# A gated attention + GLU kernel on one core: the five engines' instructions emitted into the program's main body instead of a block

## The chip, the core and the metric

The kernel runs on one core of one Trainium2 chip. The core has five engines with instruction streams of their own: TensorE (PE, with its weight loads listed apart as PEld), ScalarE (ACT), VectorE (DVE), GpSimd (POOL) and SyncE (SP). They meet only at semaphores. The metric is device time in microseconds (us) of one launch; lower is better.

## What is computed

One layer with two branches that share the input `x` (2048 rows of 512, bf16). Branch A is attention in four segments of 512 rows, with 32 heads of 16 and a running memory `M`, `z` of the earlier segments; branch B is a GLU with tanh-GELU, 1792 wide. A sigmoid gate per row mixes them.

```python
g = sigmoid((x * gate_w).sum(-1, keepdims=True))
# A, for each segment s of 512 rows, for each head:
a_dot = softmax(qs @ ks.T * 0.25 + causal_mask) @ vs
a_mem = (phi(qs) @ M) / (phi(qs) @ z + 1e-6)
o     = sigmoid(beta) * a_mem + (1 - sigmoid(beta)) * a_dot
M, z  = M + phi(ks).T @ vs, z + phi(ks).sum(rows)
a     = concat(o) @ wo
# B:
b = (gelu(x @ w_gate) * (x @ w_up)) @ w_down
out = g * a + (1 - g) * b
```

## The kernel before

`_build` (L428 on) works in two steps. First it makes a graph of some 1,200 tasks: the K, Q and V projections, the score matmuls (`fill`, L867), the exponentials (L878), the masks (L881, POOL), the products with V (`pv`, L914), the normalisation (`norm`, L937), the gate, up and down matmuls of the GLU, and the DMAs. The order in which each engine takes its tasks is written out by hand, one list for each engine (`ORDER`, L41). `Sched.schedule` (L238) walks those lists once with estimated durations; the walk decides which of four PSUM banks a group of matmuls gets. `em.plan` (L1116) and `em.finalize` (L1117) then turn the dependences into semaphore waits. All of that is done before the first instruction is emitted.

Second, it emits the streams. `Emitter.emit_stream(eng)` (L395) takes the planned list of one engine and emits, for each entry, its waits (L399) and the instruction itself. It always emits on `engmap[eng]`, the same five engine objects, wherever it is called from.

Before, the five calls stand inside `with nc.Block() as block:` (L1120). Each decorated function (L1121 to L1141) is the body of one engine, a piece of code of its own: in the program as written, each engine branches from the main body into its piece, runs it, and branches to a common end, where the block puts an all-engine barrier. In that barrier every engine drains (waits for its own instructions to retire); SP, ACT, DVE and PE each raise a semaphore; POOL waits for the four, then raises another semaphore that the four wait for. SP's body has seventeen more waits behind its last DMA (L1140, L1141): the fifteen outputs of 128 rows, and the two column pieces in which the last 128 rows are written (`sem_tail` and the last `sem_out`).

Ahead of all this the main body holds what the framework puts there when the program is opened (L1173): four constant memsets on POOL and an all-engine barrier of the same shape. The change does not touch it.

The last work of the program: PE finishes the last tile's matmuls in two column pieces (`on_x`, L1034); ACT scales the first piece into `pex` (L1048), DVE the second into `obf` (L1051), and SP writes both to memory (L1053).

Of the kernel before, what the change touches and what calls it, by code (L numbers as in the profile page):

```python
# [7 lines left out]
PE, ACT, DVE, POOL, SP = "pe", "act", "dve", "pool", "sp"  # L8
# [414 lines left out]
def build(nc, A_x, A_wq, A_wk, A_wv, A_wo, A_beta, B_x, B_w_gate, B_w_up, B_w_down, gate_w, out):  # L423
    with ExitStack() as es:
        return _build(es, nc, A_x, A_wq, A_wk, A_wv, A_wo, A_beta, B_w_gate, B_w_up, B_w_down, gate_w, out)


def _build(es, nc, A_x, A_wq, A_wk, A_wv, A_wo, A_beta, B_w_gate, B_w_up, B_w_down, gate_w, out):  # L428
# [61 lines left out]
    em = Emitter(nc, engmap)  # L490
    nsem = [0]

    def sem(name):
        nsem[0] += 1
        return es.enter_context(nc.semaphore(f"{name}_{nsem[0]}"))
# [581 lines left out]
    sem_out = [sem("so") for _ in range(16)]  # L1077
    sem_tail = sem("st")
# [38 lines left out]
    em.finalize()  # L1117
    nc._sched = S

    with nc.Block() as block:  # L1120
        @block.gpsimd  # L1121
        def _(e):
            em.emit_stream(POOL)

        @block.scalar
        def _(e):
            em.emit_stream(ACT)

        @block.vector
        def _(e):  # L1130
            em.emit_stream(DVE)

        @block.tensor
        def _(e):
            em.emit_stream(PE)

        @block.sync
        def _(e):
            em.emit_stream(SP)
            for sm in sem_out[:-1] + [sem_tail, sem_out[-1]]:  # L1140
                e.wait_ge(sm, 16)  # L1141


def bass_gated_mix__memory_aug_infini_attn__glu_gated_geglu__prompt_kernel(
# [43 lines left out]
```

## Time and profile before

| | us |
|---|---|
| median of 3 runs | 266.35 |
| lowest and highest of them | 266.17, 298.27 |
| profiled execution: span from first to last instruction | 264.8 |
| the same execution's own device time | not recorded apart from its span |

Busy time in that span: PE 256.1 us (97%), ACT 209.0 (79%), DVE 197.5 (75%), POOL 105.7 (40%). The granted TensorE clock is 1.000 throughout.

How to read the profile: "L503" is line 503 of the kernel. An engine's name with a q (SPq, PEldq) is its sequencer, the part that waits, branches and issues DMAs; its instructions aren't counted as busy. The view of one line lists every kind of instruction of that line: how many, the duration in ns (lowest/median/highest), and when the first and the last started, in us from the start of the span. The chain of waits follows the work that ended last back to what released it. A time line lists instructions as start, duration, engine, line.

### The profile page before, as it was taken

The page shows a single profiled execution, that of the slowest core. Times are in us where ns is not written, and L with a number is a line of the kernel's source. Part 1 is how long each engine was busy: PE and PEld are TensorE (multiplying, and loading weights), DVE is VectorE, ACT ScalarE, POOL GpSimd, SP SyncE. Part 2 cuts the span into 40 slices and gives each one's busy share as a digit, 9 for nine tenths or more (in the row PEclk, how much of TensorE's full clock was granted, in tenths as well). Part 3 has the DMA queues.
Part 4 walks back from the last instruction along what each step waited for, and adds up shares of the span by engine and source line. Part 5 has one row for each costly group of instructions (what it writes and reads, how often), then busy time and mean ns, then how long its engine had stood idle before and what let it go on. Part 6 is the DMA issues. An engine that isn't in the chain of part 4 may idle for free.

```text
span 264.8 us, 7355 instructions
## 1 busy us (share of the span) xinstructions
PE 256.1 (97%) x3115; PEld 117.9 (45%) x3153; DVE 197.5 (75%) x376; ACT 209.0 (79%) x179; POOL 105.7 (40%) x256
## 2 busy tenths in 40 slices
PE   8999999999999999999999999999999999999996
PEld 4644444444444434443544444343444434443453
DVE  0778788989997968889897776779887751475661
ACT  3688988998999788798877987888787777786702
POOL 8206686352600067165300274609480107362410
PEclk9999999999999999999999999999999999999999
DMA  7972216900004893320003251300000021301002
GB/s 224 310 183 43 42 24 155 284 4 0 2 9 113 227 182 73 64 82 0 2 0 59 64 140 24 83 2 20 5 2 0 2 63 41 80 2 42 22 0 82
DMA packets 32769, 18.25 MB, mean 69 GB/s; under 512 B 20576, under 2 KB 32736, under 8 KB 32736
## 3 DMA queue, kind: packets, MB, share of 16 engines
q1 hardware_dynamic: 31632, 16.73, 26.2%
q10 hardware_dynamic: 1104, 1.05, 1.3%
q8 instruction: 25, 0.41, 0.7%
q14 instruction: 8, 0.07, 0.1%
HBM read 9.84 MB, written 2.10 MB: 45 GB/s over the span
## 4 chain that ended last, share of the span: by engine, by line
PE 91%; DVE 3%; issue 2%; DMA 1%; ACT 1%; DVEq 0%; ACTq 0%
PE psW L503 71%; PE psXALL L872 8%; PE psW L920 5%; PE psXALL L503 3%; DMA hT<-in_A_x_dram 1%; PE psW L928 1%; PE psW L839 1%; DVE hT L520 1%; ACT pt L878 1%; PE psXALL L599 1%; PE psXALL L792 1%; ACT L878 0%; DVE kpad L738 0%; DVE pex L700 0%; DVE phq L698 0%
## 5 line engine op out<-in xcount | busy, mean ns | idle before, releaser
L878 ACT ACTIVATE pt<-psXALL 128x2048 bf16<-128x2048 f32 x64 | 120.1, 1876 | 27.1 <-PE psXALL L872 23.5
L881 POOL TENSOR_SCALAR_AFFINE_SELECT pt<-pt 128x256 bf16<-128x256 bf16 x128 | 58.8, 471 | 103.0 <-ACT pt L878 98.2
L503 PE MATMUL psW<-xT,wu 128*128 128x512 bf16 x217 | 53.9, 380 | 0.9 <-issue 0.6
L503 PE MATMUL psW<-wd,hT 128*128 128x512 bf16 x204 | 52.8, 380 | 1.0 <-issue 0.8
L503 PE MATMUL psW<-xT,wg 128*128 128x512 bf16 x214 | 52.1, 379 | 1.4 <-issue 0.8
L1019 DVE TENSOR_TENSOR hT<-psW,hT 128x512 bf16<-128x512 f32 x56 | 36.8, 683 | 16.5 <-PE psW L503 16.2
L881 POOL TENSOR_SCALAR_AFFINE_SELECT ptl<-ptl 128x512 bf16<-128x512 bf16 x32 | 22.5, 702 | 38.3 <-ACT ptl L878 36.6
L503 PEld LDWEIGHTS psW<-xT,wu 128*128 128x128 bf16 x224 | 20.3, 98 | 25.7 <-issue 2.7
L503 PEld LDWEIGHTS psW<-xT,wg 128*128 128x128 bf16 x224 | 20.6, 98 | 24.6 <-issue 2.1
L934 DVE STREAM_TRANSPOSE tb<-psW 128x512 f32<-128x512 f32 x32 | 21.5, 699 | 11.7 <-PE psW L928 11.5
L503 PEld LDWEIGHTS psW<-wd,hT 128*128 128x128 bf16 x210 | 19.3, 98 | 23.9 <-issue 3.0
L872 PE MATMUL psXALL<-qT,kpad 32*128 32x320 bf16 (+3 forms) x512 | 25.4, 273 | 0.0
L1003 ACT ACTIVATE hT<-psW 128x512 bf16<-128x512 f32 x28 | 15.7, 596 | 5.5 <-PE psW L503 5.4
L503 PE MATMUL psW<-xT,wk 128*128 128x512 bf16 (+1 forms) x79 | 18.9, 343 | 0.2 <-DVE mzacc L850 0.2
L920 PE MATMUL psW<-pt,vaug 128*17 128x192 bf16 (+3 forms) x512 | 18.8, 273 | 0.0
L872 PEld LDWEIGHTS psXALL<-qT,kpad 32*128 32x128 bf16 x512 | 7.6, 92 | 24.5 <-ACT pt L878 15.4
L503 PE MATMUL psW<-wv,xT 128*128 128x512 bf16 x61 | 17.8, 380 | 0.5 <-issue 0.3
L878 ACT ACTIVATE ptl<-psXALL 128x2048 bf16<-128x2048 f32 x8 | 15.0, 1876 | 3.8 <-PE psXALL L872 3.6
L503 PE MATMUL psW<-wo,oT 128*128 128x512 bf16 x54 | 15.4, 380 | 1.0 <-issue 0.8
L1068 DVE TENSOR_SCALAR ost<-psW,omgt 128x512 bf16<-128x512 f32 x9 | 6.7, 746 | 11.9 <-PE psW L503 11.9
L520 DVE CAST hT<-psW 128x512 bf16<-128x512 f32 x19 | 12.8, 684 | 3.7 <-PE psW L503 3.5
L779 POOL COPY exsT<-exs 32x4 f32<-32x4 f32 x64 | 13.9, 216 | 3.7
(104 smaller groups left out, 301.8 us busy)
## 6 DMA issues: line engine op xcount, KB each, us to landing
out_dram<-ost SPq DMA_DIRECT2D x15, 128.0 KB, 1.9
wg<-in_B_w_gate_dram SPq DMA_DIRECT2D x2, 896.0 KB, 7.6
wu<-in_B_w_up_dram SPq DMA_DIRECT2D x2, 896.0 KB, 6.9
wd<-in_B_w_down_dram SPq DMA_DIRECT2D x2, 896.0 KB, 7.0
phkt<-in_A_x_dram SPq DMA_DIRECT2D x3, 512.0 KB, 4.9
vlow<-vaug SPq DMA_DIRECT2D x8, 136.0 KB, 2.8
hT<-in_A_x_dram SPq DMA_DIRECT2D x2, 256.0 KB, 3.8
wq<-in_A_wq_dram SPq DMA_DIRECT2D x2, 256.0 KB, 5.3
```

What stands on the lines that cost most here:

```text
L503: return Instr(lambda e: e.matmul(view(), lhsT, rhs, start=first, stop=last), reads=reads, writes=[fkey if fkey is not None else g.key], e ...
L520: alts[DVE] = [Instr(lambda e: e.tensor_copy(dst(), src()), reads=reads, writes=writes, est=dve_t(n))]
L599: task(f"x0t{nm}_{u}", PE, [Instr(lambda e, k=k, a=a, u=u, k0=k0, src=src: e.transpose(src[:, k, a * 128:(a + 1) * 128], xin[:, 2 * u + a, ...
L779: cross = task(f"exsT{s}", POOL, [Instr(lambda e, g=g, c=c: e.tensor_copy(exsT[sl][32 * g:32 * g + 32, c:16:4], exs[32 * c:32 * c + 32, s4 ...
L872: instrs.append(Instr(lambda e, g=g, lhs=lhs, rhs=rhs, c0=c0, ncol=ncol: e.matmul(X[g][:, c0:c0 + ncol], lhs(32 * g), rhs(32 * g), start=T ...
L878: exp_task(s, f"exp{s}_{t}{name}", [Instr(lambda e: e.activation(dst[:], XALL[:, :].rearrange("p (g c) -> p g c", g=4), ACTF.Exp, scale=AT ...
L881: task(f"msk{s}_{t}{name}", POOL, [Instr(lambda e, view=view, pat=pat, base=base: e.affine_select(out=view, in_=view, compare_op=ALU.is_ge ...
L920: instrs.append(Instr(lambda e, t=t, q=q, kb=kb, slot=slot, c0=c0: e.matmul(gp.f32()[32 * q:32 * q + 17, 128 * kb + 64:512], Vaug[sl][:, k ...
L934: task(f"pvt{s}_{t}_{j}", DVE, [Instr(lambda e: e.transpose(Tb[:, j, :], gp.f32()[:, :]), [gp.key], [("Tb", j)], dve_t(512))], grp=gp)
L1003: lambda e, g=g, ft=ft, s=s: e.activation(hT[s % 2][:, ft, :], g.f32()[:, :], ACTF.Gelu_apprx_tanh),
L1019: task(f"Um{s}_{ft}", DVE, [Instr(lambda e, g=g, ft=ft: e.tensor_tensor(hT[sl][:, ft, :], g.f32()[:, :], hT[sl][:, ft, :], ALU.mult), [g.k ...
L1068: DVE: [Instr(lambda e, view=view, gt=gt, tile=tile: e.tensor_scalar(ostage[(4 * s + tile) % N_OST][:], view(), omgt[:, gt:gt + 1], None, ...
```

## The change

The block is gone. The same five streams are emitted one after another into the main body, and SP's waits for the outputs follow as the last instructions of SP's stream. Nothing else of the program differs: the same planned lists, the same waits, the same order on every engine. With the block go its branches and its closing barrier (a drain on each of five engines, and six semaphore instructions).

```diff
-    with nc.Block() as block:
-        @block.gpsimd
-        def _(e):
-            em.emit_stream(POOL)
-
-        @block.scalar
-        def _(e):
-            em.emit_stream(ACT)
-
-        @block.vector
-        def _(e):
-            em.emit_stream(DVE)
-
-        @block.tensor
-        def _(e):
-            em.emit_stream(PE)
-
-        @block.sync
-        def _(e):
-            em.emit_stream(SP)
-            for sm in sem_out[:-1] + [sem_tail, sem_out[-1]]:
-                e.wait_ge(sm, 16)
+    for eng in (SP, ACT, PE, DVE, POOL):
+        em.emit_stream(eng)
+    for sm in sem_out[:-1] + [sem_tail, sem_out[-1]]:
+        nc.sync.wait_ge(sm, 16)
```

## The prediction

> **What bounds the kernel now.** I read the page first, then the chain of waits, then the two ends of the program, since the change touches only those. The page:
>
> ```profile
> span 264.8 us, 7355 instructions
> PE 256.1 (97%) x3115; PEld 117.9 (45%) x3153; DVE 197.5 (75%) x376; ACT 209.0 (79%) x179; POOL 105.7 (40%) x256
> q8 instruction: 25, 0.41, 0.7%
> q14 instruction: 8, 0.07, 0.1%
> PE 91%; DVE 3%; issue 2%; DMA 1%; ACT 1%; DVEq 0%; ACTq 0%
> ```
>
> TensorE bounds it: it is busy for 97% of the span, and 91% of the chain of work that ended last is its matmuls. No edit of this change adds, removes or moves a matmul, an activation or a DMA. What can move is the start (how soon the engines begin after the opening barrier), the end (how soon the program is over after the last output has landed) and, in between, only the place of each stream in the instruction memory. I take the three in turn.
>
> **The start.** The first instructions of the program, from the view of L1173 (the framework's opening barrier) and the time line:
>
> ```profile
> L1173 POOLq EVENT_SEMAPHORE  x2: 17/17/17, 0.6 to 0.7; - x2
> L1173 ACTq DRAIN  x1: 8/8/8, 0.1 to 0.1; - x1
> L1173 SPq EVENT_SEMAPHORE  x1: 17/17/17, 0.7 to 0.7; - x1
> L1173 PEldq EVENT_SEMAPHORE  x1: 51/51/51, 0.7 to 0.7; - x1
> ...
> 0.80 0.20 POOL L561 MEMSET ident<- 128x128 bf16 x1 [0.29 <-POOLq L1173]
> 0.81 1.28 ACT L565 ACT_TABLE_LOAD   x1 [0.81 <-PEq L1173]
> 0.81 0.97 SPq L534 DMA_DIRECT2D hT<-in_A_x_dram  x2
> 0.81 0.14 PEld L590 LDWEIGHTS psW<-const-bfloat16-1.0 128*128 128x128 bf16 x2 [0.81 <-issue]
> ```
>
> The engines pass the opening barrier at 0.7 and begin the block's work at 0.80 to 0.81. The branch into the block would have to fit between. The lines of the block itself hold this:
>
> ```profile
> nothing on L1121; most used: ['L503', 'L872', 'L920', 'L928', 'L839', 'L792', 'L881', 'L399', 'L878', 'L779', 'L1019', 'L534', 'L520', 'L530', 'L599', 'L934', 'L517', 'L1003', 'L1173', 'L590', 'L946', 'L948', 'L950', 'L952', 'L767']
> L1120 POOLq EVENT_SEMAPHORE  x2: 17/17/17, 264.6 to 264.7; - x2
> L1120 POOLq DRAIN  x1: 797/797/797, 251.9 to 251.9; - x1
> L1120 PEldq DRAIN  x1: 1622/1622/1622, 260.8 to 260.8; - x1
> L1120 ACTq DRAIN  x1: 611/611/611, 261.7 to 261.7; - x1
> L1120 DVEq DRAIN  x1: 393/393/393, 262.5 to 262.5; - x1
> L1120 SPq COMPARE_BRANCH  x1: 41/41/41, 264.4 to 264.4; - x1
> L1120 SPq DRAIN  x1: 7/7/7, 264.5 to 264.5; - x1
> L1120 SPq EVENT_SEMAPHORE  x1: 17/17/17, 264.7 to 264.7; - x1
> L1120 ACTq EVENT_SEMAPHORE  x1: 17/17/17, 264.7 to 264.7; - x1
> L1120 DVEq EVENT_SEMAPHORE  x1: 21/21/21, 264.7 to 264.7; - x1
> L1120 PEldq EVENT_SEMAPHORE  x1: 51/51/51, 264.7 to 264.7; - x1
> ```
>
> The trace records a branch when one is executed: SP's at 264.4, 41 ns long. It records none at the start, on any engine, and none at the end of POOL's, ACT's, DVE's or PE's stream. So the ten branches of the source have shrunk to one; the others lead to the code that lies next on that engine anyway, and the bodies are simply entered. Removing an entry branch that isn't executed is worth 0. The bound on the other side is the gap itself: SP's wait starts at 0.7 (0.65 to 0.75 before rounding) and lasts 17 ns, its first DMA issue starts at 0.81, so the gap is 0.04 to 0.14 us, and no more than 0.1 us of it can be anything but the usual step from one instruction to the next. I take 0, with -0.1 kept for the range.
>
> [...]
>
> **The end.** The last of the chain and of SP's queue:
>
> ```profile
> 260.66 1.77 PE psXALL L503 x20
> 262.46 0.35 DVE obf L1051
> ...
> 262.84 0.33 SPq L534 DMA_DIRECT2D out_dram<-obf  x1
> ...
> out_dram<-obf SPq DMA_DIRECT2D x1, 32.0 KB, 1.4
> ...
> L1141 SPq EVENT_SEMAPHORE  x8: 28/28/28, 263.2 to 264.3; - x8
> ```
>
> PE ends at 262.4, DVE writes the last piece, SP issues its DMA at 262.84, and that lands 1.4 us later, at 264.3; the last of SP's eight wait instructions (each holds two of the seventeen waits) starts then. The seventeenth wait rides on the branch at 264.4. From here on everything belongs to the block: branch, SP's drain at 264.5, POOL's gather and release at 264.6 and 264.7, the four engines' waits at 264.7, of which PE's 51 ns end the span at 264.8.
>
> Step by step: (1) SP's branch, 41 ns, goes, and a plain wait for the same semaphore takes its place, 28 ns by the L1141 row: -0.01. (2) The stretch from the branch's end, 264.44, to 264.8 goes: -0.36. Steps 1 and 2 make 264.8 - 264.4 - 0.03 = 0.37; all starts are rounded to 0.1, so 0.3 to 0.5; I take 0.4. (3) The drains of POOL, ACT, DVE and PE go: 0. They end at 252.7, 262.3, 262.9 and 262.4, each behind its own engine's last instruction with nothing queued behind it but the barrier. What hides them is SP's wait for the output until 264.3; the landing would have to come 1.4 us earlier before the latest of them showed. (4) SP's own drain, 7 ns, is inside step 2. (5) The order of emission in the source (SP first, POOL last, instead of POOL first, SP last): 0, since each engine has its own stream and the order inside each is unchanged.
>
> What is late next is the landing of the last output, 264.3, and the wait that sees it. So the span should end at 264.4.
>
> **Between.** The streams keep their instructions but may move by a few places relative to the pieces in which code is fetched. The q8 row is that fetching: 25 packets of 0.41 MB together, one for every (3115 + 3153) / 25 = 251 PE instructions recorded. Whether PE ever waits for it shows in its waits and in its densest stretch:
>
> ```profile
> PEld psW L503 <- issue: 11.4, 54, 0.2
> PEld psXALL L872 <- issue: 4.0, 10, 0.4
> PEld psW L920 <- issue: 3.4, 11, 0.4
> ...
> 111.40:114.30 2.90, 2.90 (x108) 1.59 (x107) 2.02 (x4) 2.35 (x2) 0.41 (x1) 1.00 0.26 11
> ```
>
> After the start, no wait that nothing explains is longer than 0.4 us, and in the densest stretch that I found, 215 matmuls and weight loads in 2.9 us, PE is busy for 2.90 of 2.90. So no fetch is late now. A shift by one branch per stream, even five places, moves a fetch by 5 x 264.8 / 6268 = 0.2 us. I take 0 for it, and price the other case among the rivals.
>
> **The sum.** The page gives the profiled execution's span alone, 264.8; the median of the runs, 266.35, is 1.55 above it, which I carry over as what lies around the span. 264.8 - 0.4 + 1.55 = 265.95. The gain is 0.15%, far below 2%, which is about what a measurement of this kernel can tell from no change.
>
> **The rivals.**
>
> (a) The part around the span shrinks too. Four engines now reach their program's end at 252 to 263 instead of 264.8, and whatever closes the launch could start on them early. For it: the 1.55 us exist and no row shows what fills them. Against it: the launch is over only when the last engine is, and SP is still at 264.4. Price: between 0 and all of it, 265.95 down to 264.4; the middle is 265.2. [...]
>
> (b) Nothing is gained. What follows the program may need those same 0.4 us for its own purposes, such as draining the engines that no longer drain in the kernel. POOL's drain, at 797 ns the longest that follows its engine's work, shows that a drain isn't free, but it would run in the shadow of SP's wait. Price: 266.35.
>
> (c) The first table load moves. ACT's table load (0.81, 1.28 us) stands at the top of ACT's body. If in a single body it is put at the top of the program, ahead of the opening barrier, ACT's drain at 0.1 waits for it until 1.4, and the barrier, which now takes from the last arrival (POOL's gather, 0.6) to 0.81, releases at 1.6: +0.8. Price 265.95 + 0.8 = 266.75. Against it: the load belongs to L565, the first activation.
>
> (d) The other side: fetches become late. One mechanism, on PE: a shifted piece boundary falls so that PE runs out of fetched code before the next piece is in. [...] Against it: no late fetch now, and a shift of 0.2 us at most against 2.9 us for the densest stretch.
>
> **How the numbers follow.** Chances: the forecast 0.63; (a) 0.15; (b) 0.09; (c) 0.05; (d) 0.08. The time predicted is the forecast's, 265.95. Its own range is 265.65 to 266.15: the rounding of step 2 (0.1 either way), the -0.1 of the entry, and 0.2 for the two close runs, 266.17 and 266.35. For 8 in 10 I leave out (d) and the lower part of (a): from 265.0, just under the middle of (a), to 266.9, just over (c); that takes in (b). Faster by over 2% would need 5.3 us, and no row offers more than 0.4 + 1.55; I keep 0.01 from (a) for what lies outside every row. Slower by over 2% is (d) with more than 4 late fetches, 0.07 of its 0.08. Within 2%: 0.92.
>
> **What would show it.** Right: no instruction on the block's line; about 11 fewer instructions (12 of L1120 gone, one wait more); SP's last wait ending the span near 264.4, right behind the landing of the last output; PE's and ACT's first work still at 0.8; PE's busy time still 256. Step 3 is wrong if the span ends on an engine other than SP. Wrong at the start: the first DMA issue well off 0.81, or the table load before the opening drain (c). Wrong in between: PE waits for "issue" of over 1 us, with the q8 count unchanged (d). If the span falls by 0.4 and the time doesn't, it is (b); if the time falls by more than the span, (a).

## The result, and the profile after

The changed kernel takes 265.31 us (median of 16 runs, 264.99 to 266.71), the kernel before 266.71 (16 runs, 265.96 to 298.27): a ratio of 0.9944, with a 95% interval of 0.9923 to 0.9966; runs in a slower state, such as the one of 298.27, are left out of the ratios. That is 0.9 to 2.1 us faster, well within the 2% that the prediction called no change. In a second comparison, on one chip, the ratio was 0.9966 (0.9943 to 0.9989). Both hold the 0.95 us that the sections below account for. The time lies in the predicted range of 265.0 to 266.9, but below the forecast's own range of 265.65 to 266.15. The gain is more than twice the 0.4 us of the sum, and half of it comes from a place that the sum had carried over unchanged.

The page after, its first rows:

```profile
span 264.1 us, 7382 instructions
PE 261.1 (99%) x3153; PEld 117.6 (45%) x3153; DVE 197.5 (75%) x376; ACT 209.0 (79%) x179; POOL 105.7 (40%) x256
q8 instruction: 25, 0.41, 0.7%
```

The count rises from 7355 to 7382 though the program has shrunk: all 3153 matmuls are recorded here, and 3115 were before. 7355 + 38 = 7393, and the 11 fewer that the prediction counted make 7382. For the same reason PE's busy time reads 261.1 and not 256.1; PE does the same work.

The last of the chain of waits, the time line of SP's last DMA, and the view of L1123, where SP's last waits now stand:

```profile
260.43 1.77 PE psXALL L503 x20
262.20 0.03 issue
262.22 0.35 DVE obf L1051
...
262.60 0.33 SPq L534 DMA_DIRECT2D out_dram<-obf  x1
...
L1123 SPq EVENT_SEMAPHORE  x9: 17/28/28, 263.0 to 264.1; - x9
```

Nothing follows the last wait. By the trace's events the last output lands at 264.045 and the span ends at 264.089: 0.044 us, where before it was 0.477 (264.281 to 264.758). That is the gain at the end, 0.43 us.

The span fell by 0.67, though. The other 0.23 is in the chain's rows: PE's last piece starts at 260.43, before at 260.66. It arose in the first 7 us. The time lines there, of the kernel before and then of the changed one:

```profile
6.13 0.51 PEld L503 LDWEIGHTS psW<-xT,wk 128*128 128x128 bf16 x4
7.18 0.42 DVE L607 COPY xT<-psXALL 128x512 bf16<-128x512 bf16 x1 [0.28 <-PE psXALL L599]
```

```profile
0.80 1.28 ACT L565 ACT_TABLE_LOAD   x1 [0.80 <-PEq L1155]
0.81 0.96 SPq L534 DMA_DIRECT2D hT<-in_A_x_dram  x2
0.81 0.14 PEld L590 LDWEIGHTS psW<-const-bfloat16-1.0 128*128 128x128 bf16 x2 [0.81 <-issue]
6.03 0.37 PEld L503 LDWEIGHTS psW<-xT,wk 128*128 128x128 bf16 x4
6.95 0.42 DVE L607 COPY xT<-psXALL 128x512 bf16<-128x512 bf16 x1 [0.24 <-PE psXALL L599]
```

ACT, POOL, SP and PE's loads start as before, at 0.80 and 0.81, and the copy at L607 is already 0.23 early. Four weight loads take 0.37 us instead of 0.51: in the trace of before, loads still follow one another 107 ns apart at 6.2, and are 56 ns apart first at 6.76; in this one they are 107 ns apart up to 4.97, and 56 ns first at 5.92. The traces' own records of the granted clock begin in between, with 1.0, at 6.397 us before and at 5.905 here; ahead of them nothing is recorded, and the views print 1.00 there as well. So the clock of 1.000 throughout, given with the profile before, is known only from 6.4 us on. By the first record, TensorE's step from loads 107 ns apart to loads 56 ns apart came 0.49 us earlier in this execution, and an estimate from these figures, 0.49 x (1 - 56/107) = 0.23, is the whole difference.

That isn't the change's doing: the kernel before, profiled again (`a_block`), also has its last piece early (its last weight load starts at 261.92, the changed kernel's at 261.91, before it was 262.14), and its span is 264.5. From the copy on, in the changed kernel's profile, every stage of PE, ACT and DVE stands 0.23 us early, to within 0.02, up to the last matmul. In all fourteen profiles of this study the time from PE's 61st weight load, which starts at 10.8 to 12.9 us, to its last is 250.93 to 250.95 us.

So spans compare badly from run to run: here the head moved one by 0.23. What compares well is the distance between two events of the same run: from the last landing to the span's end, and from the span to the execution's own time, which the runs after the prediction record.

### The profile page after: what moved, and what is told of

It is laid out like the page before. It is cut to its first block, busy times and chain, and to the rows that moved or that the text cites. A ratio compares the mean times of both kernels' runs of the same rounds, so it can differ in the third digit from the quotient of the medians.

```text
span 264.1 us, 7382 instructions
## 1 busy us (share of the span) xinstructions
PE 261.1 (99%) x3153; PEld 117.6 (45%) x3153; DVE 197.5 (75%) x376; ACT 209.0 (79%) x179; POOL 105.7 (40%) x256
## 4 chain that ended last, share of the span: by engine, by line
PE 96%; DMA 1%; ACT 1%; DVE 0%; issue 0%; ACTq 0%
PE psW L503 75%; PE psXALL L872 9%; PE psW L920 6%; PE psXALL L503 3%; PE psW L928 1%; DMA hT<-in_A_x_dram 1%; PE psW L839 1%; ACT pt L878 1%; PE psXALL L792 1%; PE psXALL L599 1%; ACT L878 0%; DVE obf L1051 0%; ACTq L399 0%
## 5 line engine op out<-in xcount | busy, mean ns | idle before, releaser
L503 PE MATMUL psW<-xT,wu 128*128 128x512 bf16 x224 | 55.2, 380 | 0.0
L503 PE MATMUL psW<-xT,wg 128*128 128x512 bf16 x224 | 54.2, 380 | 0.0
L503 PE MATMUL psW<-wd,hT 128*128 128x512 bf16 x210 | 54.1, 380 | 0.0
L934 DVE STREAM_TRANSPOSE tb<-psW 128x512 f32<-128x512 f32 x32 | 21.5, 699 | 11.7 <-PE psW L928 11.5
L503 PE MATMUL psW<-wv,xT 128*128 128x512 bf16 x64 | 18.5, 380 | 0.0
L503 PE MATMUL psW<-wo,oT 128*128 128x512 bf16 x60 | 16.8, 380 | 0.0
```

Source lines behind the costliest of these rows:

```text
L503: return Instr(lambda e: e.matmul(view(), lhsT, rhs, start=first, stop=last), reads=reads, writes=[fkey if fkey is not None else g.key], e ...
L934: task(f"pvt{s}_{t}_{j}", DVE, [Instr(lambda e: e.transpose(Tb[:, j, :], gp.f32()[:, :]), [gp.key], [("Tb", j)], dve_t(512))], grp=gp)
```

## The experiments

The theory: the block cost its closing barrier and SP's branch, 0.43 us inside the span. The rivals: the part around the span shrinks as well, since four engines end early; and, what exceeds 0.43 is scatter of the head. Each kernel starts from the changed kernel, but for `a_block` and `k_no_drain`, which start from the kernel before. The part around the span, which most expectations speak of, is a run's own time less its span; spans are on record to 0.1 us, so a single run gives it to 0.05. The third column is from one profile each. `a_block` to `d_all_wait` ran on one chip, `e_last_act` to `h_last_pool` on a second, the rest on a third, each beside runs of the kernel before. Here is what they gave together, in us:

| kernel | late at the end | span's end behind last landing | part around the span: median (range, runs) |
|---|---|---|---|
| before | all five, barrier | 0.477 | 1.76 (1.67 to 1.87, 97) |
| `a_block`: before again | all five, barrier | 0.477 | 1.80 (1.72 to 1.85, 12) |
| changed | SP | 0.044 | 1.26 (1.19 to 1.36, 16) |
| `b_main`: changed again | SP | 0.044 | 1.25 (1.19 to 1.35, 12) |
| `c_main_bar` | all five, barrier | 0.296 | 1.76 (1.68 to 1.80, 12) |
| `d_all_wait` | all five | 0.079 | 1.78 (1.72 to 1.86, 12) |
| `e_last_act` | ACT | 0.059 | 1.42 (1.36 to 1.43, 10) |
| `f_last_dve` | DVE | 0.075 | 1.34 (1.30 to 1.41, 10) |
| `g_last_pe` | PE | 0.079 | 1.48 (1.46 to 1.63, 10) |
| `h_last_pool` | POOL | 0.066 | 1.81 (1.73 to 1.91, 10) |
| `i_three_wait` | SP, ACT, DVE, PE | 0.079 | 1.53 (1.46 to 1.62, 10) |
| `j_two_bars` | all five, two barriers | 0.633 | 1.76 (1.68 to 1.84, 10) |
| `k_no_drain` | all five, barrier | 0.559 | 1.78 (1.67 to 1.82, 10) |
| `l_entry` | SP | 0.045 | 1.30 (1.19 to 1.36, 10) |

The times of whole runs tell these kernels apart badly. Their ratios to the kernel before are 1.0007 for `d_all_wait`, 0.9969, 0.9972, 0.9989 and 0.9992 for `e_last_act` to `h_last_pool`, and 0.9987, 0.9999, 0.9997 and 0.9988 for `i_three_wait` to `l_entry`, each with an interval of 0.001 to 0.003 either way.

**The control and the change, on one chip.**

> The kernel before, unchanged, as a control. Theory (the closing barrier alone): ratio 1.000 to the kernel before, within 0.3%; span 264.6 to 265.1, ending on PE's wait of the barrier about 0.43 us behind the last output's wait. Rival 1 (the part around the span shrank as well): the execution's own time stands about 1.5 us above its span, where the changed kernel's stands 1.2 above. Rival 2 (the rest is scatter of the head's loads): 1.2 here too, and the spans of several runs differ by 0.2 and more.

> The changed kernel again, beside the control on one chip. Theory: 0.4 to 0.5 us under the control, ratio 0.998. Rival 1: 0.7 us or more under it, ratio 0.997 or less, with the own time 1.2 above the span. Rival 2: spans differ from the control's by 0.44 at the end and by anything from -0.3 to 0.3 in the first 10 us.

The control's ratio was 1.0007 (0.9985 to 1.0029), the change's 0.9966 (0.9943 to 0.9989); their medians 266.30 and 265.54, their lowest times 265.95 and 265.23. The part around the span is 1.80 and 1.25: rival 1 holds, beside the theory. The part around shrank by 1.80 - 1.25 = 0.55 here, and by 1.76 - 1.26 = 0.50 between the two larger sets of runs; with the middle, 0.52, the accounted gain is 0.43 + 0.52 = 0.95. The two medians differ by 0.76, since the control's spans ran from 264.2 to 266.6 and the changed kernel's from 264.0 to 266.5. That is scatter of the size that rival 2 expects, and it hits both kernels.

**One barrier, no block.**

```diff
     for sm in sem_out[:-1] + [sem_tail, sem_out[-1]]:
         nc.sync.wait_ge(sm, 16)
+    nc.all_engine_barrier()
```

> The changed kernel with one all-engine barrier behind its last waits, no block. Theory: the barrier is all that the block cost, so the end is back at 0.43 us behind the last output's wait, less what SP's branch took (41 ns and the step behind it, 0.13): 0.25 to 0.45 us over the changed kernel. A rival, that the block's form (its labels and pieces of code) costs and not its barrier: ratio as the changed kernel's, within 0.1 us.

The view of the barrier's line:

```profile
L1124 POOLq EVENT_SEMAPHORE  x2: 17/17/17, 266.1 to 266.2; - x2
L1124 POOLq DRAIN  x1: 792/792/792, 253.6 to 253.6; - x1
L1124 SPq DRAIN  x1: 7/7/7, 266.1 to 266.1; - x1
L1124 PEldq EVENT_SEMAPHORE  x1: 51/51/51, 266.2 to 266.2; - x1
```

They are the rows of the block's end, without the branch. The end is 0.296 behind the landing: the barrier costs 0.25 inside the span, and the other 0.18 of the block's 0.477 is SP's branch and the step behind it. The part around is back at 1.76, and the ratio at 1.000 (0.9983 to 1.0018). The new order of emission is still in this kernel, so it isn't what shrank the part around. Inside the span the 0.25 is at the low edge of what was expected; by the medians this kernel is 0.78 over the changed one, since the part around came back too, which this expectation hadn't counted. The rival, no cost without the block's form, is refuted; the form's own share is the 0.18.

This profile also shows one case of the scatter. Its span is 266.3, 2.2 us above the changed kernel's; 0.25 of that is the barrier, and 1.93 is there at the 61st weight load:

```profile
9.23 0.60 PE L503 MATMUL psW<-xT,wk 128*128 128x256 bf16 x4 [1.98 <-DMA wk<-in_A_wk_dram]
...
wk<-in_A_wk_dram ACTq DMA_DIRECT2D x1, 256.0 KB, 7.3
```

One load of `wk` took 7.3 us from issue to landing, where the kernel before shows 5.0 for it, and PE waited 1.98 us. From the 61st weight load on, here at 12.9 us, the run is like every other.

**All wait, nothing is exchanged.**

```diff
+    for e in (nc.scalar, nc.vector, nc.tensor, nc.gpsimd):
+        e.wait_ge(sem_out[-1], 16)
```

> The changed kernel, with ACT, DVE, PE and POOL each waiting at their end for the last output's semaphore, without barrier and drains. All five engines end together, as with the block, but nothing is exchanged. Theory: span as the changed kernel's, within 0.1 us. Rival 1 (the part around the span shrank since four engines end early): own time 0.2 to 0.4 us further above the span than the changed kernel's, like the control's. If the part around stays at 1.2, early ends don't matter.

```profile
L1125 POOLq EVENT_SEMAPHORE  x1: 17/17/17, 263.9 to 263.9; - x1
L1125 PEldq EVENT_SEMAPHORE  x1: 51/51/51, 263.9 to 263.9; - x1
```

No barrier, no drain, and the end only 0.079 behind the landing; yet the part around is 1.78, the block's, and 0.53 above the changed kernel's where rival 1 had 0.2 to 0.4. That settles rival 1: without an exchange the part around is the block's (1.78 against 1.76), so it is not the exchange that costs there, it is that engines come late.

**One engine late at a time.** The seventeen last waits move from SP to another engine, so SP ends with its last DMA issue and the other alone stays:

```diff
-        nc.sync.wait_ge(sm, 16)
+        nc.scalar.wait_ge(sm, 16)
```

and in the same way with `nc.vector`, `nc.tensor` and `nc.gpsimd`.

> The changed kernel with the seventeen last waits on ACT instead of SP: ACT alone ends late. Theory (each engine has a closing piece of its own behind its stream, and the last one done sets the time): the part around the span is ACT's piece, somewhere up to 1.78, and over the four kernels of this kind the largest is 1.78. Rival (only several late engines together cost more, in a chain from engine to engine): 1.25 here as with SP alone, within 0.1. Span 263.8 to 264.2 by both, plus what the head's loads scatter.

> The same with DVE alone late. Theory: DVE's own piece, up to 1.78; a value under 1.25 would make this a faster kernel than the changed one. Rival: 1.25 within 0.1.

> The same with PE alone late. PE's wait takes 51 ns where SP's takes 28, so the span may be 0.02 longer. Theory: PE's own piece, up to 1.78. Rival: 1.25 within 0.1.

> The same with POOL alone late. POOL's own work ends at 252.4, so it stands in the waits from then on. Theory: POOL's own piece, up to 1.78; I hold POOL for the likeliest of the four to have the largest, as its drain of 797 ns in the block's barrier was the longest behind finished work. Rival: 1.25 within 0.1.

SP 1.25, DVE 1.34, ACT 1.42, PE 1.48, POOL 1.81: the price depends on the engine that is late, and POOL's alone is the 1.76 to 1.80 of all five together. The rival, 1.25 for each, is refuted by POOL (1.73 at the lowest) and PE (1.46). SP and DVE lie close: SP's median is 1.25 to 1.30 on three sets of runs, and its range, 1.19 to 1.36, overlaps DVE's. But none is below SP's, and no other engine's wait ends sooner behind the landing than SP's 0.044, so SP is already the engine to end on: `f_last_dve`, the nearest, has 0.9972 (0.9961 to 0.9982) of the kernel before, not to be told from the changed kernel.

**Four late engines, without POOL.**

```diff
+    for e in (nc.scalar, nc.vector, nc.tensor):
+        e.wait_ge(sem_out[-1], 16)
```

> The changed kernel with ACT, DVE and PE also waiting for the last output's semaphore, POOL not. Theory (the largest closing piece among the engines that end late: SP 1.25, DVE 1.34, ACT 1.43, PE 1.49, POOL 1.81): the part around the span is PE's, 1.49 within 0.05. Rival (late engines add up): over 1.6.

1.53, for 1.49 expected: close to the largest of the four, and under the 1.6 of the rival. Without POOL among the late ones, a quarter of a microsecond of the half is back.

**Two barriers, another kind of barrier, and one at the entry.** The second barrier is one more line like that of `c_main_bar`. `k_no_drain` is the kernel before with `nc.Block(no_gpsimd_drain=True)`. `l_entry` puts this ahead of the streams:

```diff
+    with nc.Block() as block:
+        for reg in (block.gpsimd, block.scalar, block.vector, block.tensor, block.sync):
+            @reg
+            def _(e):
+                pass
     for eng in (SP, ACT, PE, DVE, POOL):
```

> Two all-engine barriers behind the last waits. Theory: the second costs inside the span what the first did, 0.25, or somewhat more since POOL's drain comes anew, so the span ends 0.55 to 0.65 behind the last landing; the part around the span stays at 1.78, since POOL was late already. Rival (the part around grows with each barrier): 2.3.

> The block again, in its form with plain drains and a barrier of semaphores alone. Theory: the drains were hidden, so nothing is won by their form: the span ends 0.45 to 0.6 behind the last landing (one more semaphore instruction per engine), the part around is 1.78. Rival (the drains cost): the end closer than 0.4.

> The changed kernel with an empty block ahead of the streams: its branches and its barrier at the entry, none at the end. Theory: a barrier costs its 0.25 wherever it stands on the path, here ahead of the first loads, so the first DMA issue moves from 0.81 to 1.05 or 1.1 and the whole run with it; the branches add nothing; the part around the span is 1.25. Rival (a branch at the entry costs a fetch of code): the first issue at 2 or later.

Two barriers: 0.633 and 1.76, both as the theory has it. The first barrier costs 0.25 inside the span, the second 0.34, and it doesn't touch the part around. The other kind of block: 0.559 and 1.78, so nothing is won, and 0.08 is lost; SP has two semaphore instructions in the view of L1120 there, where the block before has one. POOL alone has no drain there (the view of L1120 shows none; PE's, ACT's and DVE's keep their 1622, 611 and 391 ns), so POOL's drain was hidden, and the part around doesn't depend on it. The entry:

```profile
1.13 1.28 ACT L565 ACT_TABLE_LOAD   x1 [1.13 <-PEq L1120]
1.14 0.96 SPq L534 DMA_DIRECT2D hT<-in_A_x_dram  x2
```

The first issue moves from 0.81 to 1.14, 0.33, a little over the 0.25 to 0.3 that I expected and about the 0.34 of the second barrier, whose drains (7 to 41 ns each) start only behind the first. The first issue at 1.14 refutes that rival (a), which had it at 2 or later; the bodies here are empty, so a branch to a body with code in it is not tested. The part around, 1.30, is within the changed kernel's range, since the streams' ends are free again.

## Why the prediction was right, and where it was short

The class and the range were right: within 2%, and 265.31 between 265.0 and 266.9. The forecast itself was not: 265.31 lies outside its own range, 265.65 to 266.15, and inside the wider one only because that one reached down to the middle of rival (a), 265.2. The sum's gain was short: 0.4 for 0.95. In the profiled execution, the sum's 264.4 + 1.55 stands against 264.1 + 1.2; of the 0.3 in the span, 0.23 is the head's scatter, which is chance and not the change.

- **The start, taken as 0:** right. The first work stands at 0.80 and 0.81 as before. The trace records no branch at the entry, before or after, and the entry cost no time that its removal could have won. The bound of -0.1 wasn't needed.
- **The end, steps 1 and 2, taken as 0.4:** right, 0.43. Barrier 0.25, branch 0.18; the wait that remains is seen 0.044 after the landing.
- **Step 3, the drains, taken as 0:** right for the span: all four had ended by 262.9, before the landing at 264.28, and `k_no_drain` shows for POOL's that leaving it out wins nothing.
- **The sum, "1.55 above it, which I carry over as what lies around the span":** this is the step that failed, by its size and by being carried over unchanged. The profiled execution's own time wasn't shown, and subtracting its span from the median of other runs gave a wrong number: in 97 runs of the kernel before the part around is 1.76, never under 1.67. And it isn't constant: it is 1.26 after the change, because POOL, PE, ACT and DVE no longer come late: where they do, in `d_all_wait`, it is 1.78. Rival (a) named that mechanism and got a chance of 0.15; of its price, "between 0 and all of it", 0.50 to 0.55 came true. Its argument against, that "the launch is over only when the last engine is, and SP is still at 264.4", was not enough: the part around is longer with POOL alone late (1.81) than with SP (1.25), and after the change POOL's stream ends at 252.4, 11.7 us before SP's.
- **What (a) leaves open:** the late engine's name matters, by up to 0.56 us (1.81 with POOL alone late, 1.25 with SP), and with several late the part around is close to that of the costliest (1.53 for SP, ACT, DVE and PE; 1.78 for all five). Whether that is work of an engine's own or its place in some order, no run here tells apart.
- **(b)** is refuted by the ratio, **(c)** by the table load at 0.80, **(d)** by PE's 250.93 to 250.95 us in every profile. The prediction's "more than 4 late fetches" stands on its author's estimate of what one costs, which no run shows: behind the start, the longest wait of PE or its weight loads that nothing explains is 0.4 us before and after, and the q8 row has 25 packets and 0.7% in both.

What stays open: what the part behind an engine's stream, here called its closing piece, consists of, and why POOL's is the longest. It lies outside the rows that the profile shows. The runs place the difference behind the span, not ahead of it: the kernels differ in their ends alone, and `l_entry`, which differs at the start, has 1.30, within the changed kernel's range.

## What to carry to other kernels

In this kernel an all-engine barrier at the end was paid twice: its exchange behind the last landing (0.25 us, 0.43 with the branch), and a part around the span that is 0.50 to 0.55 us longer than with SP alone late. So let one engine alone wait for the outputs, the one with the shortest part around (SP here, 1.25), and keep POOL from ending late (1.81 with POOL alone late; its stream ended 11.7 us before SP's in the changed kernel). For changes under 1 us, compare distances between events of one run: in the profiles here one late load moved a whole run by 1.93 us, and the clock's step by 0.23.

## What the runs showed of the hardware beyond that

- The part around the span differs by the engine that alone is late: 1.25 us for SP, 1.34 DVE, 1.42 ACT, 1.48 PE, 1.81 POOL; with several late it is about the largest (1.53 for SP, ACT, DVE and PE, 1.78 for all five), not a sum.
- The middle, the same instruction for instruction in these kernels, took 250.93 to 250.95 us in the fourteen profiles. In them the last landing follows PE's last weight load by 2.13 to 2.14 us, so what differs apart from the ends comes from the head: in `c_main_bar` one load for which PE waited 1.98 us moved the whole run by 1.93, and between the kernel before and the changed one the instant at which TensorE's weight loads go from 107 to 56 ns apart moved it by 0.23. Runs of the kernel before whose granted clock was at least 0.999 had spans of 264.2 to 266.5; that the head makes this scatter too is likely, and not shown, as they have no traces.
- That step came at 6.40 us in one execution and at 5.91 in another, by the first record of the granted clock, with matmuls starting at 0.84 in both. What sets that instant, no run here tests.
